# Fused attention and two feed-forward layers on one core: the projection of two heads placed in the two halves of the matmul array

## The chip, the cores and the metric

The kernel runs on one core of one Trainium2 chip. The metric is the device time of one execution in microseconds (us). Before the change the median of three runs is 1108.83 us (1107.52 to 1109.21). A profile comes from one separate execution, which took 1109.95 us; its span, from the first to the last recorded instruction, is 1108.2 us.

## The reference

Three layers follow one another. The first is linear attention with an exponential feature map (4 batches, 8 heads, 576 positions, head size 64, 128 features):

```python
def phi(x):
    proj = np.einsum('bhsd,df->bhsf', x, w_phi)
    proj = proj - np.max(np.abs(proj), axis=-1, keepdims=True)
    return np.concatenate([np.exp(proj), np.exp(-proj)], axis=-1)
q_p, k_p = phi(q), phi(k)
kv = np.einsum('bhsf,bhsd->bhfd', k_p, v)
z = np.sum(k_p, axis=2)
num = np.einsum('bhsf,bhfd->bhsd', q_p, kv)
den = np.einsum('bhsf,bhf->bhs', q_p, z)[..., None] + 1e-06
return num / den
```

The second takes the real part of a two-dimensional Fourier transform of the result (over 576 positions and 512 features), adds it, normalizes each row and adds `relu(un @ w_ch1) @ w_ch2` with 2048 hidden columns. The third normalizes again, with a gain, and adds a second such pair of products. The weights of both pairs come in double precision, and all sums are in single precision.

## The kernel before, in words

**Attention.** The work goes by 16 units of two heads of one batch. A tile `qk` of a unit (lines 99 to 114) has 128 rows, 64 for each of its two heads, and nine column tiles of 128 positions: four of q, one mixed tile (64 positions of q and 64 of k), and four of k. `project` (lines 116 to 132) multiplies such a tile, which is loaded into the array as weights, with `wbd`, a 128 x 256 matrix that has `w_phi` twice on its diagonal, zeros elsewhere: one matmul gives the 128 features of both heads. It is called five times for each unit, as q0, q1, k0 and k1 (two column tiles each) and mix (one). VectorE then takes the largest magnitude (line 125) and subtracts it (line 131). Matmuls on `F32` tiles come as two pairs of a weight load and a matmul each, transposes as one pair.

`k_exp` makes the exponentials on ScalarE (line 140). `kv` (lines 143 to 158) sums over positions: 20 matmuls for a unit, each with one position tile of exponentials as weights and the 65 columns of one head's `v` (64 and a column of ones) streamed. Its last four use 64 of the array's rows. ScalarE copies the sum to `z` (line 157). `q_exp` (lines 160 to 170) transposes the projected q, one piece of 64 rows (`ptc`, line 162) and four of 128 (`ptq`, line 165), and makes its exponentials. `num` (lines 172 to 201) streams the 65 columns of `z` past ten weight loads for each head; VectorE divides and writes the result to `ub` and `uc`.

**Order.** The list `rounds` (line 559) gives the order of these stages in a round; `num` belongs to the unit before, `load` to the second next. The stage `dft` stands for pieces of other work that are tied to a round (lines 532 to 544): the Fourier transform of finished batches (`fold`, `seq_stage`, `dim_stage`) and the decoding of the first weights. A planner that simulates the engines orders the instructions of each engine's queue from this program order and from what each waits for; the queues themselves run in order.

**PSUM.** Results of TensorE go to rings of banks by tag (line 48): `p` has two banks (projections, `ptc`, and later `ph`), `t` two (transposes), `n` four (`pk`, `px`, `pb`, `pd`, and later `acc`).

**Weights.** A block of raw weights (512 KB) is requested by SyncE in `fetch` (lines 314 to 323) into one of `RAW = 2` buffers `wraw`, and `decode` (lines 345 to 361) makes two single-precision tiles of it on ScalarE and VectorE; `decode` calls `fetch` itself. The first eight blocks are decoded in the rounds of line 532, the others at fixed places of the feed-forward loop (lines 493 to 498).

**Feed-forward.** From about 290 us on, `mm1` (line 427) and `mm2` (line 443) run for two layers, four groups of hidden columns and five chunks of rows; they are not touched by the change except by the rings and by the weights.

Of the kernel before, what the change touches and what calls it, by code (L numbers as in the profile page):

```python
# [19 lines left out]
F = 128  # L20
# [11 lines left out]
def fused_kernel(ctx, tc, qk_c, v_c, w_phi, w1s, w2s, g_ln, cs_c, cd_c, perm_c, out):  # L32
# [14 lines left out]
    def ps_tile(tag, shape, name):  # L47
        return psum.tile(shape, F32, tag=tag, bufs={"p": 2, "t": 2, "n": 4}[tag], name=name)
# [48 lines left out]
    KT = {"q0": 0, "q1": 2, "mix": 4, "k0": 5, "k1": 7}  # L97

    def load(u):
        qk = apool.tile([P, 9, P], F32, tag="qk", bufs=2, name="qk")  # L100
        vv = apool.tile([P, 5, 2, D + 1], F32, tag="vv", bufs=2, name="vv")
        def part(a, b):
            nc.sync.dma_start(qk[:, a:b], qk_c[u, :, a * P : b * P].rearrange("p (t c) -> p t c", c=P))

        if u == 0:
            part(5, 7)
            load_consts()
            part(7, 9)
            part(4, 5)
# [4 lines left out]
        st[u]["qk"], st[u]["v"] = qk, vv  # L114

    def project(u, name):
# [7 lines left out]
        mx = apool.tile([P, 2 * n], F32, tag="mx", bufs=4, name="mx")  # L124
        nc.vector.tensor_reduce(out=mx, in_=pp, op=ALU.max, axis=AX.X, apply_absolute_value=True)  # L125
        if name == "k0":
            st[u]["mx"] = mx[:, 0:1]
            if u == 0:
                load_dft_consts()
        t = bpool.tile([P, 2 * n, F], F32, tag="pm" + name[0], bufs=2, name="pm")  # L130
        nc.vector.tensor_tensor(out=t, in0=pp, in1=mx.unsqueeze(2).to_broadcast([P, 2 * n, F]), op=ALU.subtract)  # L131
        st[u]["pm", name] = t

    def k_exp(u, name):
        t = st[u]["pm", name]
        n = 1 if name == "mix" else 2
        r = slice(64, P) if name == "mix" else slice(0, P)
        e = apool.tile([P, 2 * n, 2, F], F32, tag=f"ek{n}", bufs=2, name="ek")
        for sgn in range(2):
            nc.scalar.activation(e[r, :, sgn], t[r], AF.Exp, scale=1.0 - 2.0 * sgn)  # L140
        st[u]["ek", name] = e

    def kv(u):
        pk = ps_tile("n", [P, 4, D + 1], "pk")
        first = True
        for t in range(5):
            e = st[u]["ek", ("k0", "k1", "mix")[t // 2]]
            r = slice(64, P) if t == 4 else slice(0, P)
            for j in range(2):
                for sgn in range(2):  # L150
                    nc.tensor.matmul(  # L151
                        pk[:, 2 * j + sgn, :], e[r, 2 * (t % 2) + j, sgn], st[u]["v"][r, t, j],
                        start=first, stop=(t == 4), skip_group_check=True,
                    )
                    first = False
        z = bpool.tile([P, 4, D + 1], F32, tag="z", bufs=2, name="z")
        nc.scalar.copy(z, pk)
        st[u]["z"] = z

    def q_exp(u, j):  # L160
        ptc = ps_tile("p", [P, 64], "ptc")
        nc.tensor.transpose(ptc, st[u]["pm", "mix"][0:64, j, :], ident[0:64, 0:64])
        pt = ps_tile("t", [P, 4, P], "ptq")
        for t in range(4):
            nc.tensor.transpose(pt[:, t, :], st[u]["pm", f"q{t // 2}"][:, 2 * (t % 2) + j, :], ident)  # L165
# [137 lines left out]
    weights = {}  # L303
    wpools = {}
# [9 lines left out]
    def fetch(layer, g, n):  # L314
# [8 lines left out]
        return raw  # L323
# [21 lines left out]
    def decode(layer, g, n):  # L345
# [4 lines left out]
        raw = fetch(layer, g, n)  # L350
# [123 lines left out]
    def moe(last_dft):  # L474
# [44 lines left out]
    nc.vector.memset(ub[0][:, 0], 0.0)  # L519
    warm = ps_tile("n", [P, DM], "warm")  # L520
# [11 lines left out]
    for n, step in enumerate((2, 3, 4, 7, 8, 11, 15, 17)):  # L532
        at(step, decode, 0, 0, n)
# [3 lines left out]
    for b in range(B - 1):  # L537
# [9 lines left out]
        "k0": lambda u: (project(u, "k0"), k_exp(u, "k0")),  # L547
        "k1": lambda u: (project(u, "k1"), k_exp(u, "k1")),
        "mix": lambda u: (project(u, "mix"), k_exp(u, "mix")),
        "q0": lambda u: project(u, "q0"),  # L550
        "q1": lambda u: project(u, "q1"),
# [8 lines left out]
        ("k0", 0), ("num0", -1), ("k1", 0), ("mix", 0), ("num1", -1), ("q0", 0),  # L560
        ("q1", 0), ("load", 2), ("dft", 0), ("e0", 0), ("kv", 0), ("e1", 0),
# [103 lines left out]
```

## Time and profile before

| | |
|---|---|
| median of the runs | 1108.83 us |
| profiled execution, its span | 1109.95 us, 1108.2 us |
| TensorE (PE) busy | 1086.3 us, 98% |
| weight loads (PEld) busy | 927.9 us, 84% |
| VectorE (DVE) busy | 615.0 us, 55% |
| ScalarE (ACT) busy | 340.5 us, 31% |
| GpSimd (POOL) busy | 45.3 us, 4% |

A row of a group of instructions gives line, engine, operation, written and read tiles, rows x columns of the array in use (128*64, 64*128), shape and count, then busy us and the mean ns of one, then idle time of the engine before it. A row of the timeline gives the start in us, the length in us from the first start to the last end, the engine and the instructions that it merges (x count). Matmuls are pipelined: of several in a row the distance between starts is the length less that of one, divided by the count less one. A row of windows gives for a stretch its length and the busy time of PE, PEld, DVE, ACT and POOL with counts, then PEclk, the granted clock of TensorE as a share of full speed, then the DMA share and GB/s. A row of waits gives who waited for whom: us in total, times, the longest.

### The profile page before, as it was taken

To read this page: it belongs to the slowest core of one execution; us is meant where nothing else is said; L and a number is where in the kernel's file an instruction comes from. 1 tells how busy PE (TensorE), PEld (TensorE's weight loads), DVE (VectorE), ACT (ScalarE), POOL (GpSimd) and SP (SyncE) were. 2 spreads that over 40 slices of the span, in tenths; PEclk is the share of its full clock that TensorE was granted. 3 is DMA by queue.
4 is the path that set the end of the run, shared out by engine and by line. 5 is a ranking of instruction groups with operands and counts; after the bars stand their busy time and mean duration, and the time that the engine had idled before them with its cause. 6 is when DMAs were issued, how large, how long until landed. Compare 5 with 4: busy or idle time off the path is not lost.

```text
span 1108.2 us, 14381 instructions
## 1 busy us (share of the span) xinstructions
PE 1086.3 (98%) x5806; PEld 927.9 (84%) x5806; DVE 615.0 (55%) x1315; ACT 340.5 (31%) x682; POOL 45.3 (4%) x53
## 2 busy tenths in 40 slices
PE   9899999999999999999999999999999999999996
PEld 7789989999788888888888788888878888888885
DVE  5897586774879476238327755762383264222131
ACT  4545454454435131113113343521231132011110
POOL 1000020300210000000000000000000000000010
PEclk9899999999999999999999999999999999999998
DMA  7452121110003122003101300220031011000111
GB/s 257 144 161 77 46 60 42 57 46 1 1 1 114 39 76 76 1 1 114 39 1 50 103 1 1 64 89 1 1 115 38 1 39 38 1 1 10 48 48 67
DMA packets 19755, 57.26 MB, mean 52 GB/s; under 512 B 2728, under 2 KB 3432, under 8 KB 19432
## 3 DMA queue, kind: packets, MB, share of 16 engines
q1 hardware_dynamic: 18536, 51.01, 14.3%
q0 software_dynamic: 1008, 5.19, 1.3%
q8 instruction: 46, 0.75, 0.3%
q14 instruction: 21, 0.17, 0.1%
q10 hardware_dynamic: 144, 0.13, 0.0%
HBM read 51.60 MB, written 4.72 MB: 51 GB/s over the span
## 4 chain that ended last, share of the span: by engine, by line
PE 86%; DVE 8%; DMA 4%; ACT 2%; issue 1%; POOLq 0%; POOL 0%; DVEq 0%; SPq 0%; ACTq 0%
PE acc L443 33%; PE ph L427 32%; PE pk L151 5%; PE px L181 5%; PE pp L121 5%; DMA wraw<-in_moe_w_ch 4%; PE pb L260 2%; PE ptq L165 1%; PE ptx L409 1%; PE pd L287 1%; DVE wm L342 1%; DVE wm L337 1%; DVE xx L215 1%; DVE wm L334 0%; DVE hl L431 0%
## 5 line engine op out<-in xcount | busy, mean ns | idle before, releaser
L427 PE MATMUL ph<-xth,wh 128*128 128x512 f32 (+1 forms) x640 | 236.2, 369 | 0.7 <-ACT xth L411 0.7
L427 PE MATMUL ph<-xtl,wh 128*128 128x512 f32 (+1 forms) x640 | 235.8, 368 | 0.0
L427 PE MATMUL ph<-xth,wl 128*128 128x512 f32 (+1 forms) x640 | 235.7, 368 | 0.0
L431 DVE SCALAR_TENSOR_TENSOR hl<-ph,hh 128x512 fp32r<-128x512 f32 (+1 forms) x160 | 101.5, 634 | 232.7 <-ACT hh L430 232.4
L430 ACT ACTIVATE hh<-ph 128x512 fp32r<-128x512 f32 (+1 forms) x160 | 88.4, 554 | 461.6 <-PE ph L427 456.4
L443 PE MATMUL acc<-wl,hh 128*128 128x512 f32 x576 | 224.2, 390 | 0.0
L443 PE MATMUL acc<-wh,hh 128*128 128x512 f32 x576 | 221.2, 391 | 2.5 <-ACT hh L430 2.5
L443 PE MATMUL acc<-wh,hl 128*128 128x512 f32 x576 | 195.3, 390 | 0.0
L427 PEld LDWEIGHTS ph<-xth,wh 128*128 128x128 f32 x640 | 120.4, 188 | 21.8 <-ACT xth L411 0.9
L427 PEld LDWEIGHTS ph<-xtl,wh 128*128 128x128 f32 x640 | 120.5, 188 | 20.7
L427 PEld LDWEIGHTS ph<-xth,wl 128*128 128x128 f32 x640 | 120.6, 188 | 20.0
L445 DVE TENSOR_TENSOR u<-acc,u 128x512 f32<-128x512 f32 x128 | 81.2, 682 | 94.3 <-PE acc L443 94.1
L443 PEld LDWEIGHTS acc<-wh,hh 128*128 128x128 f32 x576 | 108.1, 188 | 25.4 <-ACT hh L430 3.6
L443 PEld LDWEIGHTS acc<-wl,hh 128*128 128x128 f32 x576 | 108.2, 188 | 22.1
L443 PEld LDWEIGHTS acc<-wh,hl 128*128 128x128 f32 x576 | 107.1, 188 | 21.2
L121 PE MATMUL pp<-wbd,qk 128*128 128x256 f32 x288 | 80.2, 398 | 3.2 <-ACT eq L168 1.9
L151 PEld LDWEIGHTS pk<-vv,ek 128*128 128x128 f32 (+1 forms) x640 | 77.6, 191 | 5.2 <-ACT ek L140 1.8
L151 PE MATMUL pk<-vv,ek 128*128 128x65 f32 (+1 forms) x640 | 80.1, 273 | 0.8 <-ACT ek L140 0.6
L181 PEld LDWEIGHTS px<-z,eq 128*128 128x128 f32 (+1 forms) x640 | 76.3, 186 | 3.9 <-issue 0.3
L181 PE MATMUL px<-z,eq 128*128 128x65 f32 (+1 forms) x640 | 76.1, 268 | 0.0
L125 DVE TENSOR_REDUCE mx<-pp 128x4 f32<-128x512 f32 (+1 forms) x80 | 50.5, 631 | 45.5 <-PE pp L121 44.8
L140 ACT ACTIVATE ek<-pm 128x512 f32<-128x512 f32 (+1 forms) x96 | 48.2, 551 | 44.5 <-DVE pm L131 44.2
(100 smaller groups left out, 954.2 us busy)
## 6 DMA issues: line engine op xcount, KB each, us to landing
wraw<-in_moe_w_ch SPq DMA_DIRECT2D x64, 512.0 KB
vv<-in_v SPq DMA_DIRECT2D x16, 325.0 KB
qk<-in_qk SPq DMA_DIRECT2D x15, 320.0 KB
qk<-in_qk SPq DMA_DIRECT2D x16, 256.0 KB
out<-u SPq DMA_DIRECT2D x8, 256.0 KB
cs<-c_seq POOLq DMA_DIRECT2D x1, 1920.0 KB, 10.3
cd<-c_dim POOLq DMA_DIRECT2D x1, 1032.0 KB, 13.0
out<-uc SPq DMA_DIRECT2D x4, 126.0 KB
```

Of the source, the lines that this page charges most:

```text
L121: nc.tensor.matmul(pp[:, 2 * i : 2 * i + 2, :], qk[:, KT[name] + i], wbd.rearrange("p h f -> p (h f)"), start=True, stop=True)
L125: nc.vector.tensor_reduce(out=mx, in_=pp, op=ALU.max, axis=AX.X, apply_absolute_value=True)
L140: nc.scalar.activation(e[r, :, sgn], t[r], AF.Exp, scale=1.0 - 2.0 * sgn)
L151: nc.tensor.matmul(pk[:, 2 * j + sgn, :], e[r, 2 * (t % 2) + j, sgn], st[u]["v"][r, t, j], start=first, stop=(t == 4), skip_group_check=True,)
L165: nc.tensor.transpose(pt[:, t, :], st[u]["pm", f"q{t // 2}"][:, 2 * (t % 2) + j, :], ident)
L181: nc.tensor.matmul(px[0 : c.stop - c.start, t, :], e[:, sgn, c], z[:, 2 * j + sgn], start=(t == 0 and sgn == 0), stop=(sgn == 1), skip_gro ...
L260: nc.tensor.matmul(o, a, c, start=(n == 0), stop=(n == len(mm) - 1), skip_group_check=(m == 2))
L427: nc.tensor.matmul(ph[:, 0:n], a[:, kk, sl], x[:, kk], start=(i == 0), stop=(i == 11))
L430: nc.scalar.activation(hh[:, 0:n], ph[:, 0:n], AF.Relu)
L431: nc.vector.scalar_tensor_tensor(out=hl[:, 0:n], in0=ph[:, 0:n], scalar=0.0, in1=f32(hh[:, 0:n]), op0=ALU.max, op1=ALU.subtract)
L443: nc.tensor.matmul(acc, x[:, sl], w[:, f], start=(f == 0 and n == 0), stop=(f == 3 and n == 2))
L445: nc.vector.tensor_tensor(out=x, in0=acc, in1=x, op=ALU.add)
```

## The change

The two heads of a unit are projected by separate matmuls. For q and for k each, four position tiles times two heads make eight matmuls; each uses the 64 array rows of its head, and streams the 128 columns of `w_phi` instead of 256. The results of the two heads go to two banks, and `center` (the maximum and the subtraction) is called once for each head. The mixed tile stays as it was. The first unit's k tiles are now loaded by one request.

The ring `p` gets three banks, `n` three, and `ptc` moves from `p` to `n`. `kv` streams 128 columns instead of 65, 63 of which belong to the other head and are not used; `z` is copied by two instructions; `num` streams 102 columns instead of 65, of which 65 are used.

`fetch` is taken out of `decode`. For the first group it is called one round before its `decode`; for the other groups the next block's `fetch` stands in front of a block's `decode`. The number of buffers stays two.

```diff
-        return psum.tile(shape, F32, tag=tag, bufs={"p": 2, "t": 2, "n": 4}[tag], name=name)
+        return psum.tile(shape, F32, tag=tag, bufs={"p": 3, "t": 2, "n": 3}[tag], name=name)
...
         if u == 0:
-            part(5, 7)
+            part(5, 9)
             load_consts()
-            part(7, 9)
             part(4, 5)
...
     def project(u, name):
-        n = 1 if name == "mix" else 2
+
         qk = st[u]["qk"]
-        pp = ps_tile("p", [P, 2 * n, F], "pp")
-        for i in range(n):
-            nc.tensor.matmul(
-                pp[:, 2 * i : 2 * i + 2, :], qk[:, KT[name] + i], wbd.rearrange("p h f -> p (h f)"), start=True, stop=True
-            )
...
+        pp = [ps_tile("p", [P, 4, F], "pp") for _ in range(2)]
+        for i in range(4):
+            for j in range(2):
+                r = slice(j * D, (j + 1) * D)
+                nc.tensor.matmul(pp[j][:, i], qk[r, KT[name] + i], wbd[r, j], start=True, stop=True)
+        for j in range(2):
+            mx = center(u, name, j, pp[j])
...
     def kv(u):
-        pk = ps_tile("n", [P, 4, D + 1], "pk")
+
+        pk = ps_tile("n", [P, 4, P], "pk")
...
                     nc.tensor.matmul(
-                        pk[:, 2 * j + sgn, :], e[r, 2 * (t % 2) + j, sgn], st[u]["v"][r, t, j],
+                        pk[:, 2 * j + sgn, :], e[r, sgn], st[u]["v"][r, t].rearrange("p h d -> p (h d)")[:, 2 * j : 2 * j + P],
                         start=first, stop=(t == 4), skip_group_check=True,
...
-        z = bpool.tile([P, 4, D + 1], F32, tag="z", bufs=2, name="z")
-        nc.scalar.copy(z, pk)
+        z = zs[u % 2]
+        for j in range(2):
+            c = slice(j * (D - 1), j * (D - 1) + D + 1)
+            nc.scalar.copy(
+                z[:, 2 * j * (D + 1) : 2 * (j + 1) * (D + 1)].rearrange("p (s d) -> p s d", s=2),
+                pk[:, 2 * j : 2 * j + 2, c],
+            )
...
+    ZW = 102
+    zs = [bpool.tile([P, 3 * (D + 1) + ZW], F32, name=f"z{i}") for i in range(2)]
...
-        ptc = ps_tile("p", [P, 64], "ptc")
+        ptc = ps_tile("n", [P, 64], "ptc")
...
-        px = ps_tile("n", [P, 5, D + 1], "px")
+        px = ps_tile("n", [P, 5, ZW], "px")
...
-                    px[0 : c.stop - c.start, t, :], e[:, sgn, c], z[:, 2 * j + sgn],
+                    px[0 : c.stop - c.start, t, :], e[:, sgn, c],
+                    z[:, (2 * j + sgn) * (D + 1) : (2 * j + sgn) * (D + 1) + ZW],
...
-        for k in range(8):
-            side.setdefault((0, 2 + k // 4, 2 * (k % 4)), []).append(partial(decode, 0, 1, k))
-        for p in range(1, 7):
-            for k in range(8):
-                at = (p, k // 2, 1 + 4 * (k % 2))
-                side.setdefault(at, []).append(partial(decode, (p + 1) // 4, (p + 1) % 4, k))
+        def weight_steps(p, times):
+
+            blocks = [((p // 4, p % 4, k), t) for k, t in enumerate(times)]
+            side.setdefault(blocks[0][1], []).insert(0, partial(fetch, *blocks[0][0]))
+            for (a, t), nxt in zip(blocks, blocks[1:] + [None]):
+                side[t] = side.get(t, []) + ([partial(fetch, *nxt[0])] if nxt else []) + [partial(decode, *a)]
+
+        weight_steps(1, [(0, 2 + k // 4, 2 * (k % 4)) for k in range(8)])
+        for p in range(2, 8):
+            weight_steps(p, [(p - 1, k // 2, 1 + 4 * (k % 2)) for k in range(8)])
...
     for n, step in enumerate((2, 3, 4, 7, 8, 11, 15, 17)):
+        at(step - 1, fetch, 0, 0, n)
         at(step, decode, 0, 0, n)
...
     rounds = (
-        ("k0", 0), ("num0", -1), ("k1", 0), ("mix", 0), ("num1", -1), ("q0", 0),
-        ("q1", 0), ("load", 2), ("dft", 0), ("e0", 0), ("kv", 0), ("e1", 0),
+        ("k", 0), ("num0", -1), ("mix", 0), ("num1", -1), ("q", 0),
+        ("load", 2), ("dft", 0), ("e0", 0), ("kv", 0), ("e1", 0),
     )
```

## Rows read from the trace of the kernel before

**Rows 1.** The page's first part: busy us, share of span, instructions.

```profile
PE 1086.3 (98%) x5806; PEld 927.9 (84%) x5806; DVE 615.0 (55%) x1315; ACT 340.5 (31%) x682; POOL 45.3 (4%) x53
```

**Rows 2.** Windows: attention, and the feed-forward part.

```profile
0.00:290.00 290.00, 282.18 (x2006) 255.32 (x2007) 211.66 (x520) 142.56 (x333) 32.05 (x39) 0.99 0.26 85
...
340.00:1108.00 768.00, 755.58 (x3557) 632.71 (x3556) 361.86 (x694) 176.55 (x305) 7.80 (x8) 1.00 0.13 41
```

**Rows 3.** Waits of TensorE, over the whole span.

```profile
PE acc L443 <- ACT hh L430: 2.5, 2, 1.4
PE ptc L162 <- ACT eq L168: 2.0, 1, 2.0
PE pp L121 <- ACT eq L168: 1.9, 4, 0.6
```

**Rows 4.** Groups by line with shapes apart: projections and the two sums.

```profile
L121 PE MATMUL pp<-wbd,qk 128*128 128x256 f32 x288 | 80.2, 398 | 3.2 <-ACT eq L168 1.9 <-PE pp L121 0.7 <-issue 0.6
...
L181 PE MATMUL px<-z,eq 128*128 128x65 f32 x576 | 70.0, 272 | 0.0
L151 PE MATMUL pk<-vv,ek 128*128 128x65 f32 x512 | 62.9, 272 | 0.8 <-ACT ek L140 0.6
...
L181 PE MATMUL px<-z,eq 128*64 128x65 f32 x64 | 7.3, 234 | 0.0
```

**Rows 5.** Timeline of TensorE: one projection matmul, three, and eleven of a sum.

```profile
182.85 0.38 PE L121 MATMUL pp<-wbd,qk 128*128 128x256 f32 x1
...
114.48 0.81 PE L121 MATMUL pp<-wbd,qk 128*128 128x256 f32 x3
...
115.75 1.39 PE L181 MATMUL px<-z,eq 128*128 128x65 f32 x11
```

**Rows 6.** Timeline of TensorE: four matmuls with 64 weight columns.

```profile
19.14 0.45 PE L181 MATMUL px<-z,eq 128*64 128x65 f32 x4
```

**Rows 7.** Timeline of TensorE: a 64-row transpose between 128-row instructions.

```profile
93.75 0.50 PE L151 MATMUL pk<-vv,ek 128*128 128x65 f32 x3
94.19 0.27 PE L162 MATMUL ptc<-perm,pm 64*128 64x64 f32 x1
94.39 0.44 PE L165 MATMUL ptq<-perm,pm 128*128 128x128 f32 x2
```

**Rows 8.** Timeline: a transpose in rows 0-63 among matmuls in rows 64-127.

```profile
181.48 0.61 PE L151 MATMUL pk<-vv,ek 64*128 64x65 f32 x4
181.82 0.27 PE L162 MATMUL ptc<-perm,pm 64*128 64x64 f32 x1
181.93 0.38 PE L151 MATMUL pk<-vv,ek 64*128 64x65 f32 x2
...
181.82 0.14 PEld L162 LDWEIGHTS ptc<-perm,pm 64*128 64x128 f32 x1
```

**Rows 9.** Timeline: the one such place with another order of starts.

```profile
29.20 0.13 PEld L162 LDWEIGHTS ptc<-perm,pm 64*128 64x128 f32 x1
29.22 0.19 PEld L151 LDWEIGHTS pk<-vv,ek 64*128 64x128 f32 x1
29.23 0.24 PE L162 MATMUL ptc<-perm,pm 64*128 64x64 f32 x1
```

**Rows 10.** Window of the one low stretch of the clock in attention.

```profile
46.30:53.10 6.80, 4.94 (x15) 3.93 (x15) 5.15 (x11) 4.45 (x13) 0.00 (x0) 0.50 0.44 152
```

**Rows 11.** Windows: a stretch with decoding, and one with little beside attention.

```profile
70.00:90.00 20.00, 19.41 (x145) 17.60 (x144) 19.74 (x52) 10.91 (x24) 5.01 (x2) 1.00 0.41 126
160.00:200.00 40.00, 39.92 (x293) 36.63 (x294) 23.08 (x61) 20.23 (x53) 0.00 (x0) 1.00 0.20 62
```

**Rows 12.** Waits of SyncE's queue; timeline of ScalarE in the feed-forward part.

```profile
SPq L322 <- DVE wm L342: 694.4, 62, 96.5
...
622.37 0.67 ACT L329 ACTIVATE wm<-wraw 128x512 f32<-128x512 f32 x1 [1.79 <-DMA wraw<-in_moe_w_ch]
```

**Rows 13.** Groups by line: the copy of the sum.

```profile
L157 ACT COPY z<-pk 128x260 f32<-128x260 f32 x16 | 6.0, 377 | 21.1 <-PE pk L151 21.1
```

More of the change, by code (lines that the diff above doesn't have):

```diff
@@ L96, in fused_kernel @@
     st = [dict() for _ in range(NUNIT)]
-    KT = {"q0": 0, "q1": 2, "mix": 4, "k0": 5, "k1": 7}
+    KT = {"q": 0, "mix": 4, "k": 5}
     def load(u):
@@ L114, in load, with center @@
         st[u]["qk"], st[u]["v"] = qk, vv
+    def center(u, name, j, pp):
+        n = pp.shape[1]
+        mx = apool.tile([P, n], F32, tag="mx", bufs=4, name="mx")
+        nc.vector.tensor_reduce(out=mx, in_=pp, op=ALU.max, axis=AX.X, apply_absolute_value=True)
+        t = bpool.tile([P, n, F], F32, tag="pm" + name[0], bufs=2, name="pm")
+        nc.vector.tensor_tensor(out=t, in0=pp, in1=mx.unsqueeze(2).to_broadcast([P, n, F]), op=ALU.subtract)
+        st[u]["pm", name, j] = t
+        return mx
@@ L126, in project @@
[L126 to L136, printed above, removed]
+        pp = [ps_tile("p", [P, 4, F], "pp") for _ in range(2)]
@@ new lines, in project, with project_mix @@
+        for i in range(4):
[4 more added lines that the diff above has]
+            mx = center(u, name, j, pp[j])
+            if name == "k":
+                st[u]["mx"] = mx[:, 0:1]
+                if u == 0:
+                    load_dft_consts()
+    def project_mix(u):
+        pp = ps_tile("p", [P, 2, F], "pp")
+        nc.tensor.matmul(pp, st[u]["qk"][:, KT["mix"]], wbd.rearrange("p h f -> p (h f)"), start=True, stop=True)
+        center(u, "mix", 0, pp)
@@ L137, in k_exp @@
+    def k_exp(u, name, j):
+        t = st[u]["pm", name, j]
         r = slice(64, P) if name == "mix" else slice(0, P)
-        e = apool.tile([P, 2 * n, 2, F], F32, tag=f"ek{n}", bufs=2, name="ek")
+        e = apool.tile([P, t.shape[1], 2, F], F32, tag="ek" + name[0], bufs=2, name="ek")
         for sgn in range(2):
             nc.scalar.activation(e[r, :, sgn], t[r], AF.Exp, scale=1.0 - 2.0 * sgn)
-        st[u]["ek", name] = e
+        st[u]["ek", name, j] = e
     def kv(u):
-        pk = ps_tile("n", [P, 4, D + 1], "pk")
+        pk = ps_tile("n", [P, 4, P], "pk")
@@ L155, in kv @@
                     first = False
-        z = bpool.tile([P, 4, D + 1], F32, tag="z", bufs=2, name="z")
-        nc.scalar.copy(z, pk)
+        z = zs[u % 2]
[5 more added lines that the diff above has]
+            )
         st[u]["z"] = z
+    ZW = 102
+    zs = [bpool.tile([P, 3 * (D + 1) + ZW], F32, name=f"z{i}") for i in range(2)]
     def q_exp(u, j):
-        ptc = ps_tile("p", [P, 64], "ptc")
-        nc.tensor.transpose(ptc, st[u]["pm", "mix"][0:64, j, :], ident[0:64, 0:64])
+        ptc = ps_tile("n", [P, 64], "ptc")
+        nc.tensor.transpose(ptc, st[u]["pm", "mix", 0][0:64, j, :], ident[0:64, 0:64])
         pt = ps_tile("t", [P, 4, P], "ptq")
         for t in range(4):
-            nc.tensor.transpose(pt[:, t, :], st[u]["pm", f"q{t // 2}"][:, 2 * (t % 2) + j, :], ident)
+            nc.tensor.transpose(pt[:, t, :], st[u]["pm", "q", j][:, t, :], ident)
         e = bpool.tile([P, 2, S], F32, tag="eq", bufs=2, name="eq")
@@ L303, in fused_kernel @@
     weights = {}
+    raws = {}
     wpools = {}
@@ L349, in decode @@
         wh, wl = weights[layer, g][w]
-        raw = fetch(layer, g, n)
+        raw = raws.pop((layer, g, n))
         m = to_float(raw)
@@ L519, in fused_kernel @@
     nc.vector.memset(ub[0][:, 0], 0.0)
+    for z in zs:
+        nc.vector.memset(z[:, 4 * (D + 1) :], 0.0)
     warm = ps_tile("n", [P, DM], "warm")
@@ L546, in fused_kernel @@
         "load": load,
[L547 to L551, printed above, removed]
+        "k": lambda u: (project(u, "k"), k_exp(u, "k", 0), k_exp(u, "k", 1)),
+        "mix": lambda u: (project_mix(u), k_exp(u, "mix", 0)),
+        "q": lambda u: project(u, "q"),
         "e0": lambda u: q_exp(u, 0),
```

6 lines of the change are left out of this document (2 added, 4 removed).

## Prediction

> **What bounds the kernel now.** I read the first part of the page, then the windows by stage, then the waits of TensorE, then its timeline for the distances between starts. The page says that TensorE is busy for 1086.3 of 1108.2 us [rows 1]; the windows say the same of each stage: 282.2 of the 290 us of attention, 755.6 of 768 of the feed-forward part [rows 2]. Busy time overlaps from one matmul to the next, so I check it by the waits: the longest of TensorE are 2.5, 2.0 and 1.9 us in total [rows 3]. The reader is to see that hardly any time goes to waiting: TensorE's stream of instructions sets the time, and an edit counts by what it does to the distance between their starts. Only attention changes there: 288 projection matmuls, 640 of `px`, and 640 of `pk`, of which 512 with all rows [rows 4].
>
> **Projection: the streams.** One projection matmul lasts 0.38 us and three 0.81, so starts are (0.81 - 0.38)/2 = 0.215 us apart for 256 columns [rows 5]. A run of eight (two calls of `project`) takes 8 x 0.215 = 1.72 us. Streaming a column thus costs 0.215/256 = 0.00084 us: 128 columns 0.108, 102 columns 0.086, 65 columns 0.055. Yet eleven `px` matmuls of 65 columns take 1.39 us with 0.27 for the last: starts 0.112 apart [rows 4, 5]. So there the load of 128 weight columns sets the pace, at 0.112; with 64 weight columns four take 0.45, the last 0.23 [rows 4, 6], about 0.07 apart.
>
> The changed projection has 16 matmuls in that run, each with its own load of 128 columns and a stream of 0.108. Loads set 0.112 in each half of the array, eight for each half. If the halves run beside one another, the run takes 8 x 0.112 + one offset of 0.112 = 1.01 us, a gain of 0.71; if not, 16 x 0.112 = 1.79, a loss of 0.07, or a little less loss where part overlaps. These are the two ends.
>
> **Projection: changes between whole and half array.** A 64-row transpose between 128-row work starts 0.21 us after the matmul before it, and the next starts 0.20 after it, where 0.11 is usual, and the one after that is 0.165 behind (0.44 - 0.27) where 0.11 is usual [rows 4, 7]. So a change costs 0.09 + 0.055 = 0.15 us. A longer stream ahead of it drains longer (102 or 128 columns for 65: 0.03 to 0.05), so I take 0.18. Each run needs a change in and one out: 0.36 of the 0.71. There are 32 such runs (q and k of 16 units): 32 x 0.35 = 11.2 us gained. Where a run stands beside `ptc` or the last `pk` matmuls, which are 64-row too, a change is saved; at most one for each run, 4.8 us. I take none.
>
> **Do the halves overlap?** At 181.8 us `ptc`, in rows 0 to 63, starts in the middle of `pk` matmuls in rows 64 to 127. The last `pk` before it starts at 181.48 + 0.61 - 0.27 = 181.82, the next at 181.93: they keep their 0.11, and `ptc` ends with the former at 182.09. Its load, too, starts at 181.82 between theirs [rows 8]. So loads and streams of two halves do run together, for one transpose. What isn't shown is that they stay together in a row. The two passes of head 0 come before those of head 1, so the second matmul of head 0 waits for the first; the load for head 1 has to pass that waiting matmul. In 13 of the 14 places like this the other half's load starts only after the matmul before it has started, as here. In one, a `pk` load starts at 29.22 ahead of the `ptc` matmul at 29.23 that stands before it in the program [rows 9]. The 13 loads carry a semaphore wait, which the projection's don't; so I side with the one, at about six in ten.
>
> The Trainium skill, "TensorE: Matmul & The Clock Gate", Part 3 (The mechanism), says that the engine pulls a weight load ahead of matmuls whose row group doesn't conflict. By that rule the run is the 1.01 us above in every case; by the 13 places alone it would be the first rival below. No run here shows the rule for two loads in a row.
>
> **Wider sums.** For `pk` (128 columns, 0.108) and the 576 full `px` (102 columns, 0.086) the load still sets 0.112: nothing, hidden under the load. If a load could not run under a stream, each would cost up to 0.05 more, some 60 us over 1216; but the projections' 0.215 holds stream and load in one [rows 5], so I exclude it. The 64 `px` with 64 weight columns go from 0.07 or less to 0.086: 64 x 0.02 = 1.3 us. At the changes there are now (in and out of the last `pk`, into the short `px`) the longer stream drains: 48 x 0.05 = 2.4. Together 3.7 us lost.
>
> **Rings.** The waits of `ptc` and `pp` on `eq` (3.9 us) [rows 3] are for the ring `p`, where `ptc` held a bank; there they go. What is late next is the ring `n`, which loses a bank and takes in `ptc`, beside `px`, `pk`, `pb` and pairs of `pd`. I put new waits between 0 and 4 us and take 2, a gain of 2. The clock was granted at half for 6.8 us from 46.3 on [rows 10], right after the 2.0 us wait, which costs 3.4 us of stream. If the wait goes, so may that; I take 2 of the 3.4, and as the other end one more such stretch.
>
> **Raw weights.** SyncE waits 694 us, 62 times, for VectorE to free a `wraw` buffer [rows 12], and there are two buffers before and after. A request further ahead in the queue waits for the same buffer, so I take nothing. What it could bring at most is the 2.5 us that TensorE waits on `hh` [rows 3], where ScalarE stood 1.79 us on a block [rows 12]; lost could be as much, where a request that waits for its buffer delays the `qk` request behind it in SyncE's queue.
>
> **VectorE.** Its work is the same but for the pieces: 211.7 of 290 us in attention [rows 2]. But in stretches with decoding or transform work it is full, 19.7 of 20 us; elsewhere it has room, 23.1 of 40 [rows 11]. Some 80 of the 290 us are like the former, and a quarter of the net gain (7.5) is lost there: 2 us. The second copy to `z` adds at most the 0.38 of the present one for each unit on ScalarE [rows 13]; `num` needs it a round later, so nothing. If ScalarE were late it would be 16 x 0.38 = 6 us. The first unit's one request is hidden by the warm-up matmuls; at worst 0.7 us.
>
> **The sum**, from the profiled 1109.95 us: - 11.2 + 3.7 - 2 - 2 + 2 = -9.5, so 1100.4; the runs' median is 1.1 below the profiled execution, so 1099.5.
>
> **The rivals.**
> 1. The halves don't stay together: either the load waits behind the blocked matmul, or the streams take turns. Then the run is 1.79 us and the changes between whole and half array are pure loss: 32 x (0.07 + 0.36) = 13.8, with the sums 17.5, less 4 for rings and clock: 13.5 slower, 1122 on the runs' scale. It decides from about 1.4 us for a run. For: the 13 places. Against: rows 9, and that streams do overlap.
> 2. VectorE takes the place of TensorE. It must subtract a bank pair before the next projection, in three banks; if it holds the gain down to the quiet third of attention, 2.5 us are left of 7.5 and the rings give nothing back: 1106 to 1109. For: full stretches. Against: 27% of attention idle. The Trainium skill, "TensorEngine Tiling (Array Packing)", PSUM Bottleneck, says that array packing speeds up the matmuls and not the emptying of PSUM, which may become the bound; the full stretches agree, their neighbours don't.
> 3. All goes well: no low clock, no ring waits, 2.5 us of the weights' wait gone, some changes shared: 1109.95 - 11.2 + 3.7 - 3.9 - 3.4 - 2.5 - 3 = 1090, 1089 on the runs' scale.
>
> **How the numbers follow.** Forecast 0.50 (1093 to 1105), rival 1 0.28 (1113 to 1127), rival 2 0.12, rival 3 0.10 (1087 to 1093). A measurement of this kernel tells 0.2%, 2.2 us, from no change. Faster: 0.49 + 0.10 + 0.03 = 0.62; same 0.01 + 0.07 = 0.08; slower 0.28 + 0.02 = 0.30. The range leaves out half of rival 1 and most of rival 3: 1091 to 1121; the forecast's own is 1093 to 1105.
>
> **What would show it.** In the changed profile a run of 16 projection matmuls should take about 1.0 us from first to last start (rival 1: 1.7 or more), starts before and after it 0.2 to 0.3 apart, `px` and `pk` still 0.112, `ptc` and `pp` without waits on `eq`, attention ending 8 to 10 us earlier, and the feed-forward part as long as now, with its two waits. I am wrong if the run's length is near 1.7, if `px` and `pk` starts move beyond 0.12, if new low stretches of the clock appear, or if waits on `n` banks exceed 4 us.

## The result, and the profile after

The changed kernel takes 1121.2 us (median of four runs, 1120.33 to 1121.8) against 1109.02 for the kernel before on the same chip: a ratio of 1.0105, 95% interval 1.0089 to 1.0121. It is 12 us slower where 9.5 us faster were forecast. Executions differ in how long TensorE's clock stands at its lower level, so one profiled execution can lie several us from its kernel's median, and ratios leave out executions over 1.5% above their kernel's fastest. The profiled one here took 1121.2.

The first part of the page and the two windows, answering to [rows 1, 2]:

```profile
PE 1093.5 (98%) x6062; PEld 930.4 (83%) x6062; DVE 617.5 (55%) x1317; ACT 337.6 (30%) x698; POOL 45.1 (4%) x58
...
0.00:290.00 290.00, 275.74 (x2160) 244.02 (x2161) 197.10 (x495) 133.58 (x335) 25.90 (x39) 0.98 0.29 96
340.00:1119.00 779.00, 772.46 (x3640) 647.58 (x3638) 387.02 (x749) 186.02 (x323) 10.06 (x11) 1.00 0.13 42
```

TensorE now stands idle for 14.3 of the first 290 us, where it was 7.8 before. The waits of TensorE, answering to [rows 3], name the place:

```profile
PE ptc L181 <- DMA perm<-c_perm: 6.8, 1, 6.8
PE pp L132 <- DVE pm L121: 3.7, 3, 1.4
PE pb L280 <- DVE xs L246: 1.9, 1, 1.9
PE ph L448 <- DVE hl L452: 1.9, 1, 1.9
...
PE ptc L181 <- DVE rr L313: 1.2, 1, 1.2
```

No `ptc` or `pp` waits for `eq` any more, as forecast; but the longest wait is one that the prediction does not contain. The DMA issues of the page and the one instruction tell why (first two: count, KB each, us to landing; third: ns that issuing took, first and last start in us):

```profile
cs<-c_seq POOLq DMA_DIRECT2D x2, 1920.0 KB, 8.2
cd<-c_dim POOLq DMA_DIRECT2D x2, 1032.0 KB, 9.2
...
L75 SPq DMA_DIRECT2D perm<-c_perm x2: 327/334/340, 4.3 to 9.5; - x2
```

The tables are requested twice. `load_dft_consts()` stood in `project`, guarded by `name == "k0"`; the change moved it into the loop over the two heads, where `name == "k"` and `u == 0` hold twice. The first transpose must wait until the second copy of `perm`, issued at 9.5 us, has landed among 3 MB of tables that are sent again. The timeline of TensorE at that place, and the windows of the low clock, the first of which begins within that wait:

```profile
17.43 0.34 PE L181 MATMUL ptc<-perm,pm 64*128 64x64 f32 x1 [6.82 <-DMA perm<-c_perm]
```
```profile
12.40:22.60 10.20, 5.17 (x21) 4.63 (x22) 0.02 (x1) 0.68 (x4) 1.45 (x4) 0.50 1.04 415
155.80:159.10 3.30, 3.30 (x18) 3.30 (x17) 3.30 (x9) 0.91 (x2) 3.30 (x3) 0.50 0.02 7
312.80:316.10 3.30, 3.30 (x14) 2.58 (x13) 3.15 (x10) 0.75 (x2) 0.74 (x2) 0.50 0.00 0
```

The clock was granted at half (1.2 of 2.4 GHz) in three stretches of 16.8 us together, beside one behind the last matmuls in every kernel; before it was one of 6.8 [rows 10].

And the projections? The forecast hung on runs of 16 half-array matmuls in 1.01 us. Timeline of TensorE, one run early in the attention and two halves of later ones:

```profile
33.16 1.16 PE L132 MATMUL pp<-wbd,qk 64*128 64x128 f32 x16
...
54.84 1.16 PE L132 MATMUL pp<-wbd,qk 64*128 64x128 f32 x8
...
72.00 1.16 PE L132 MATMUL pp<-wbd,qk 64*128 64x128 f32 x8
```

With 0.27 for the last matmul, the first row is 16 matmuls in 0.89 us from first to last start, the starts alternately 7 and 105 ns apart but for one step of 206 near the beginning: the halves do run beside one another. The others are 8 matmuls in the same 0.89 us, the first two 0.213 apart and the rest 0.112: one head alone. The program order alternates the heads, but the planner gives out a matmul when its bank is free, and a projection takes two of the three banks of ring `p`, with `mix` between. Only seven stretches have just 16 in a row, four of them in 0.89 us. Of the 256 starts that would come under 40 ns behind another if all were paired, 113 do. That the order of the queue parts the halves is tested below (3).

**A ledger.** Busy times overlap, so I add up distances: for each kernel, the distance from the start of each matmul in the trace to the start of the next, put down to the tile of the first. In stretches at half clock (a distance belongs to one if it starts in it) half of each distance goes to the tile and half to "low clock". Outside them, a distance over 0.33 us leaves 0.2 with the tile and the rest in "waits"; the warm-up is left whole. "Ends" is what lies before the first and behind the last start. So each column adds up to the span of the one profiled execution (us):

| | before | after | single request | whole array | pair of banks | before, wide | before, end |
|---|---|---|---|---|---|---|---|
| `pp` | 62.8 | 62.2 | 63.9 | 66.5 | 42.5 | 61.3 | 62.5 |
| `ptc`, `ptq` | 22.2 | 20.7 | 20.3 | 19.5 | 22.3 | 22.3 | 22.1 |
| `pk` | 73.2 | 75.8 | 74.9 | 75.1 | 74.9 | 76.6 | 73.3 |
| `px` | 70.0 | 75.0 | 74.9 | 73.8 | 75.1 | 73.0 | 70.2 |
| `pb`, `pd`, `ptx` | 57.9 | 59.1 | 59.0 | 58.3 | 58.4 | 58.2 | 57.9 |
| `ph`, `acc`, warm-up | 792.4 | 792.3 | 792.2 | 792.2 | 792.3 | 792.3 | 792.3 |
| low clock | 2.7 | 6.0 | 10.2 | 3.2 | 9.9 | 1.6 | 3.3 |
| waits | 14.9 | 19.5 | 12.0 | 8.5 | 25.2 | 15.0 | 16.8 |
| ends | 12.0 | 8.8 | 8.9 | 8.9 | 12.0 | 11.9 | 7.0 |
| span | 1108.2 | 1119.4 | 1116.2 | 1105.9 | 1112.6 | 1112.2 | 1105.4 |

The columns from the third on are experiments, below, in this order: the tables requested once (1), projections over all 128 rows and a pair of banks for them (3), the kernel before with the wide sums (4) and with another end (5).

### The profile page after: what moved, and what is told of

The parts are those of the page before. It is cut to its first block, busy times and chain, and to the rows that moved or that the text cites. A ratio compares the mean times of both kernels' runs of the same rounds, so it can differ in the third digit from the quotient of the medians.

```text
span 1119.4 us, 14918 instructions
## 1 busy us (share of the span) xinstructions
PE 1093.5 (98%) x6062; PEld 930.4 (83%) x6062; DVE 617.5 (55%) x1317; ACT 337.6 (30%) x698; POOL 45.1 (4%) x58
## 4 chain that ended last, share of the span: by engine, by line
PE 93%; DVE 3%; DMA 2%; ACT 1%; issue 0%; POOLq 0%; ACTq 0%; DVEq 0%
PE ph L448 35%; PE acc L464 35%; PE pk L162 7%; PE px L200 6%; PE pp L132 4%; PE pb L280 2%; PE ptq L184 1%; PE ptx L430 1%; DMA perm<-c_perm 1%; PE pp L142 1%; DVE u L317 1%; PE pd L307 1%; DVE xx L235 0%; DMA wraw<-in_moe_w_ch 0%; ACT ek L150 0%
## 5 line engine op out<-in xcount | busy, mean ns | idle before, releaser
L464 PE MATMUL acc<-wl,hh 128*128 128x512 f32 x576 | 220.7, 390 | 0.0
L464 PE MATMUL acc<-wh,hh 128*128 128x512 f32 x576 | 218.6, 391 | 0.0
L464 PE MATMUL acc<-wh,hl 128*128 128x512 f32 x576 | 211.4, 390 | 0.0
L466 DVE TENSOR_TENSOR u<-acc,u 128x512 f32<-128x512 f32 x128 | 85.6, 687 | 137.2 <-PE acc L464 136.9
L162 PE MATMUL pk<-vv,ek 128*128 128x128 f32 (+1 forms) x640 | 82.3, 286 | 0.3 <-ACT qs L311 0.2
L200 PE MATMUL px<-z,eq 128*128 128x102 f32 (+1 forms) x640 | 77.4, 276 | 0.3 <-ACT z L170 0.3
L200 PEld LDWEIGHTS px<-z,eq 128*128 128x128 f32 (+1 forms) x640 | 72.9, 186 | 4.5 <-ACT z L170 0.5
L132 PE MATMUL pp<-wbd,qk 64*128 64x128 f32 x512 | 59.1, 290 | 4.2 <-DVE pm L121 3.7
L132 PEld LDWEIGHTS pp<-wbd,qk 64*128 64x128 f32 x512 | 49.0, 189 | 14.8 <-issue 9.3
```

The costliest lines, as they stand in the source:

```text
L132: nc.tensor.matmul(pp[j][:, i], qk[r, KT[name] + i], wbd[r, j], start=True, stop=True)
L162: nc.tensor.matmul(pk[:, 2 * j + sgn, :], e[r, sgn], st[u]["v"][r, t].rearrange("p h d -> p (h d)")[:, 2 * j : 2 * j + P], start=first, st ...
L200: nc.tensor.matmul(px[0 : c.stop - c.start, t, :], e[:, sgn, c], z[:, (2 * j + sgn) * (D + 1) : (2 * j + sgn) * (D + 1) + ZW], start=(t == ...
L464: nc.tensor.matmul(acc, x[:, sl], w[:, f], start=(f == 0 and n == 0), stop=(f == 3 and n == 2))
L466: nc.vector.tensor_tensor(out=x, in0=acc, in1=x, op=ALU.add)
```

## Experiments

Each was timed in turns with the kernel before; the ratio is to that, with its 95% interval. It is not the quotient of the medians.

**1. The double request.** Two kernels from both sides.

```diff
-                if u == 0:
+                if u == 0 and j == 0:
                     load_dft_consts()
```

> The changed kernel, but the cosine tables, alt and perm are requested once, after the first head's maximum of unit 0, not once for each head. Theory A (the second request is the loss: 6.8 us of the first transposes on perm, the half clock of 10.2 us behind it, and everything after it moved back): 8 to 11 us faster than the changed kernel, 1110 to 1113 us, the first unit's last px sum 9 to 10 us earlier; the feed-forward keeps its 3 to 4 us. Theory B (rival 1 of the prediction, the runs that are split by head and their mode changes are the loss, the second request lies beside other work): 0 to 3 us faster, 1118 to 1121 us, the delay of the first unit made up for by the runs of the later units in which TensorE waits less.

Measured: 1116.1 us, 1.0065 (1.0044 to 1.0087), 5.1 us faster than the changed kernel.

```diff
             if u == 0:
                 load_dft_consts()
+                load_dft_consts()
```

> The kernel before, but cosine tables, alt and perm are requested twice in unit 0, one request right behind the other, as in the changed kernel. Theory A: 7 to 11 us slower than the kernel before, 1116 to 1120 us, the first transposes waiting 5 us or more for perm. Theory B: within 3 us of the kernel before, 1109 to 1112 us.

Measured: 1114.35 us, 1.0081 (1.0049 to 1.0112), 5.3 us slower than before. Its first waits show the same place, shorter:

```profile
PE ptc L163 <- DMA perm<-c_perm: 2.4, 1, 2.4
```

So by the medians the double request costs about 5 us from both sides. By the ratios its size is less sure: 4.4 us less on the changed kernel, 5.4 to 12.4 more on the kernel before. The first is short of theory A's 8 us, the second beyond theory B's 3. The other 7 us of the loss have another cause.

**2. The raw blocks requested ahead,** alone on the kernel before, with the function `weight_steps` of the change, and taken out of the kernel with the single request.

```diff
-        raw = fetch(layer, g, n)
+        raw = raws.pop((layer, g, n))
...
+        at(step - 1, fetch, 0, 0, n)
```

> The kernel before with one part of the change alone: raw weight blocks are requested one round before they are decoded. Theory A (it is this that gives the feed-forward back 3 to 4 us, the two waits for weights near 622 and 694 us being gone): 2 to 4 us faster than before, 1105 to 1107 us, with the attention as long as before. Theory B (the shorter feed-forward comes from the different start of the stage, or the wider rings): within 1 us of before, 1108 to 1110 us.

Measured: 1108.7 us, 0.9992 (0.9975 to 1.0009).

```diff
         wh, wl = weights[layer, g][w]
+        fetch(layer, g, n)
         raw = raws.pop((layer, g, n))
...
-        at(step - 1, fetch, 0, 0, n)
```

> The kernel of the single request of the tables, with the request of each raw weight block back beside its decoding: so the halves, the wide sums and the rings alone. Theory A: 2 to 4 us slower than the kernel of the single request (1112 to 1116 us), the feed-forward waiting for weights again near 622 and 694 us after its start of the stage; and 3 to 6 us slower than the kernel before, since the runs that are split by head gain nothing and pay mode changes and longer sums. Theory B (the request ahead is worth nothing): within 1 us of the kernel of the single request.

Measured: 1118.47 us, 1.0079 (1.0058 to 1.0101), an interval that overlaps that of the single request. Theory A falls: on the kernel before nothing can be measured, and the waits of `acc` for `hh` [rows 3] stay there, 1.8 us, while they are gone in the kernel without the early request. (In the kernel before they stand at 622 and 828 us, not near 694.) What shortens the end of the kernel is something else (5).

**3. The halves.** First without them: each head's projection with all 128 rows, 128 columns a matmul, all else as with the single request.

```diff
-                r = slice(j * D, (j + 1) * D)
-                nc.tensor.matmul(pp[j][:, i], qk[r, KT[name] + i], wbd[r, j], start=True, stop=True)
+                nc.tensor.matmul(pp[j][:, i], qk[:, KT[name] + i], wbd[:, j], start=True, stop=True)
```

> The kernel of the single request, but each head's projection takes all 128 rows (its weights' other half is zero), 128 columns a matmul, so nothing runs in halves; rings, sums and raw requests stay. Theory A (the halves as they now run, mostly one head at a time, gain no more than their changes of mode cost): within 3 us of the kernel of the single request, 1113 to 1118 us, a run of 16 at 16 x 0.112 = 1.8 us. Theory B (the halves do gain several us, and something else costs more): 5 to 10 us slower, 1121 to 1126 us.

Measured: 1107.78 us, 0.9993 (0.9981 to 1.0006): 8.3 us faster than with halves. Both theories missed; neither had the halves as a loss of that size. The ledger splits it: without halves `pp` costs 2.6 us more, `ptc` and `ptq` 0.8 less, the low clock takes 7.0 less and waits 3.5 less. The two profiles are one execution each; the granted clock of all executions goes the same way, on the mean 0.991 of six with halves and 0.996 of twelve without. The low stretches in the kernel with halves:

```profile
10.90:17.70 6.80, 6.80 (x32) 6.13 (x30) 2.29 (x4) 2.55 (x9) 0.00 (x0) 0.50 0.96 389
92.80:96.20 3.40, 3.40 (x19) 3.40 (x18) 3.39 (x8) 0.00 (x0) 0.35 (x1) 0.50 0.67 200
229.40:236.10 6.70, 6.14 (x25) 5.12 (x25) 6.59 (x19) 2.27 (x6) 1.71 (x3) 0.50 0.00 0
301.00:304.40 3.40, 3.31 (x8) 2.64 (x9) 3.40 (x8) 0.00 (x0) 0.00 (x0) 0.50 0.00 0
```

TensorE is nearly always busy in them, but its starts are about twice as far apart: 32 in the first 6.8 us. They follow distances of 1.7, 1.2, 1.5 and 2.3 us between starts. The whole-array kernel has two stretches of 3.4, behind distances of 1.9 and 2.3.

Then with all halves paired: both heads in one tile of two banks.

```diff
-        bufs={"p": 3, "t": 2, "n": 3}[tag]
+        bufs={"p": 1, "t": 2, "n": 4}[tag]
...
-        pp = [ps_tile("p", [P, 4, F], "pp") for _ in range(2)]
+        pp = ps_tile("p", [P, 2, 4, F], "pp")
...
-        ph = ps_tile("p", [P, 512], "ph")
+        if not phs:
+            phs.append(ps_tile("p", [P, 2, 512], "ph"))
+        ph = phs[0][:, f % 2]
```

> The kernel of the single request, with both heads of a projection in one tile of two banks, so that no order can part them (rings p one tile of two banks, t 2, n 4 as before the change; the mix projection is in ring n, the feed-forward keeps two banks for ph). Theory A (the prediction's 11 us of the projections failed because most runs were given out one head at a time, at 0.112 us a matmul): every run of 16 takes 0.9 to 1.0 us from first to last start, the projections fall by 10 to 14 us of TensorE's time, 1102 to 1108 us. Theory B (the halves are paid for elsewhere: half clock, VectorE, changes of mode): the runs do become short, but 1112 to 1118 us, TensorE waiting for VectorE's pm at the projections instead.

Measured: 1180.24 us, 1.0627 (1.0604 to 1.0651). This one misled: I had put `ph` of the feed-forward into two slices of a single tile, and `acc` then waits 39.1 us for `hh`. Mended, with two banks for `ph` from a pool opened when the attention's is closed:

```diff
-        if not phs:
-            phs.append(ps_tile("p", [P, 2, 512], "ph"))
-        ph = phs[0][:, f % 2]
+        ph = ps_tile("h", [P, 512], "ph")
```

> As the kernel with both heads in one tile of two banks, but with the feed-forward's ph in two banks of its own, opened when the attention's are closed, so that the 39 us of acc waiting for hh go. Theory A (with all runs paired the halves gain, what is left against the kernel before is half clock and waits for the one pair of banks): attention 5 to 7 us longer than before, feed-forward as before, 1113 to 1118 us. Theory B (the pair itself is worth its 11 us once nothing else is changed): 1102 to 1108 us.

Measured: 1114.91 us, 1.0051 (1.003 to 1.0073), theory A. Its projections, beside those of the changed kernel, each in the first 290 us (busy us, mean ns; idle before):

```profile
L135 PE MATMUL pp<-wbd,qk 64*128 64x128 f32 x512 | 41.3, 296 | 10.9 <-issue 7.3 <-DVE pm L124 2.5 <-PE px L203 1.1
```
```profile
L132 PE MATMUL pp<-wbd,qk 64*128 64x128 f32 x512 | 59.1, 290 | 4.2 <-DVE pm L121 3.7 <-PE pp L142 0.5
```

Here 27 runs are whole, 22 of them in 0.89 us. Against the kernel before with wide sums, the nearest with the same banks, `pp` falls by 18.8 us; waits rise by 10.2 and low clock by 8.3. Nearly nothing is left: the span is 0.4 us longer, the median 1.4 shorter. One of the waits, on VectorE and TensorE:

```profile
159.93 1.01 DVE L122 TENSOR_REDUCE mx<-pp 128x4 f32<-128x512 f32 x2
...
161.06 1.00 DVE L124 TENSOR_TENSOR pm<-pp,mx 128x512 f32<-128x512 f32 x2
...
161.84 0.92 PE L135 MATMUL pp<-wbd,qk 64*128 64x128 f32 x11 [3.02 <-issue]
```

The page finds no releaser, but the neighbours point to one: the first of the two subtractions is the last from the only pair (the other is the mixed tile's); it ends at 161.73, and TensorE starts the next pair at 161.84. So I gave it two pairs, with two banks left in ring `n`, and `mix` and `ptc` in ring `t`:

```diff
-        bufs={"p": 1, "h": 2, "t": 2, "n": 4}[tag]
+        bufs={"p": 2, "h": 2, "t": 2, "n": 2}[tag]
```

> As the kernel with the pair of banks and ph in banks of its own, but two pairs (4 banks) for the projections, mix and ptc in ring t, 2 banks left in ring n. Theory A (with one pair, TensorE's 17 us at the projections are given back as waits of the next projection for VectorE, 7 to 9 us, and as half clock): the waits of pp fall under 3 us, 1105 to 1111 us. Theory B (VectorE's reductions or two banks for the sums bound the stage instead): the waits move to px and pk, 1113 us or more.

Measured: 1124.3 us, 1.013 (1.0096 to 1.0164). `pp` waits less, 3.3 us in the ledger instead of 12.4, so the one pair of banks was what it waited for. But the waits of the ledger rise from 25.2 to 33.9, now mostly at `ph` (8.6), `acc` (6.9) and `pd` (4.7), and `pp` itself takes 47.8 us, with 13 whole runs for 27. So theory B has the time, but at other tiles: `acc` and `pd` have two banks instead of four; why `ph` waits is not shown. In neither of the two splits of the eight banks do the pairs keep what they save.

**4. The wide sums,** taken out of the kernel with the single request:

```diff
-        pk = ps_tile("n", [P, 4, P], "pk")
+        pk = ps_tile("n", [P, 4, D + 1], "pk")
...
-    ZW = 102
+    ZW = 65
```

> The kernel of the single request, with the sums back at 65 columns. Theory A (the wide sums cost what the prediction gave them, 3.7 us): 2 to 5 us faster, 1111 to 1114 us, px of 64 rows back at 0.06 us. Theory B (their columns lie under the weight loads, which take 0.111 us at either width): within 1.5 us of it, 1115 to 1117 us. Theory C (the wide sums hold TensorE's clock up, and narrow ones let it fall): slower, 1118 to 1122 us, with more than 20 us at the lower clock.

Measured: 1172.42 us (1151.17 to 1180.83), 1.0438 (1.0379 to 1.0497). Theory C, far beyond its size. Two of its stretches:

```profile
11.00:79.00 68.00, 65.50 (x320) 59.91 (x318) 45.15 (x107) 27.31 (x63) 0.30 (x2) 0.50 0.50 165
...
110.00:157.70 47.70, 45.80 (x230) 43.17 (x231) 22.28 (x48) 12.85 (x32) 2.35 (x1) 0.50 0.12 39
```

In all 164 us were granted at half clock, 81 us of loss in the ledger. The same edit with whole-array projections of 128 columns:

> Projections with all rows at 128 columns, and sums of 65 columns. Theory A (the granted clock falls where halves and narrow sums come together; whole-array projections keep it up): under 25 us at half clock, 1103 to 1110 us, as the kernel with wide sums or 3 us faster. Theory B (it is the narrow sums alone that let the clock fall, whatever the projections are, once these stream 128 and no longer 256 columns): over 60 us at half clock, 1135 us or more.

Measured: 1110.9 us (1102.69 to 1113.82), 0.9986 (0.9958 to 1.0014), with 23.9 us at half clock in the profiled execution of 1112.08: theory A, but for the time. At a mean granted clock of 0.996 or 0.997, which five of the twelve executions had, it took 1102.7 to 1104.5 us, some 3 us less than the whole-array kernel with wide sums and near the prediction's term of 3.7. The wide sums alone, on the kernel before (`kv`, `zs` and `num` as in the change):

```diff
-        px = ps_tile("n", [P, 5, D + 1], "px")
+        px = ps_tile("n", [P, 5, ZW], "px")
```

> The kernel before with the wide sums alone. Theory A (the prediction's term): 2 to 5 us slower, 1111 to 1114 us, px of 64 rows 0.087 us instead of 0.06, the rest of the sums at 0.112 us as before. Theory B (the wide sums cost nothing that shows, since they take away the half-clock stretch of 6.8 us, 3.4 us): within 1.5 us of the kernel before.

Measured: 1116.32 us, 1.0063 (1.0044 to 1.0081); the profiled execution is 4.0 us above that of before, the medians 7.6; theory A is the nearer, and too low. `pk` and `px` cost 6.3 us more in the ledger, the low clock 1.1 less. The 64 short `px` start 0.105 us apart on the mean instead of 0.077 (1.3 us in all), and the full `pk` and `px` 0.114 and 0.111 instead of 0.1085. That mean hides two kinds: nine in ten start 0.11 apart with either width, but 76 full ones, each the second of its group, started about 0.06 us behind the first before, and now start 0.087 (`px`) or 0.108 and more (`pk`) behind it. Two such, before and with wide sums:

```profile
101.92 0.33 PE L181 MATMUL px<-z,eq 128*128 128x65 f32 x2
```
```profile
100.56 0.36 PE L190 MATMUL px<-z,eq 128*128 128x102 f32 x2
```

With 0.275 for the second, the starts are 0.057 and 0.087 apart: there the stream sets the distance, not the load. These places are about half of the 6.3 us.

**5. The rings, and the end.**

```diff
-        bufs={"p": 2, "t": 2, "n": 4}[tag]
+        bufs={"p": 3, "t": 2, "n": 3}[tag]
```

> The kernel before with the rings alone changed: p 3 banks and n 3 instead of 2 and 4 (ptc and everything else as before). Theory A (the shorter feed-forward of the changed kernel comes from the third bank of ring p, which ph uses there): the two waits of acc for hh are gone and the feed-forward is 2.5 to 4 us shorter; if the attention keeps its length, 1105 to 1107 us. Theory B (it comes from something else in the change): the waits stay, 1108 to 1110 us, or slower where three banks of ring n hold the attention up (1111 or more).

Measured: 1107.45 us (1105.16 to 1127.18), 0.9998 (0.9971 to 1.0026). Inconclusive in time: the profiled execution took 1117.47 with 30.7 us at half clock. But the two waits of `acc` for `hh` are gone with the rings alone, and so is part of the end: 7.3 us from the last matmul's start to the end of the span, 10.5 before. With wide sums as well:

> The kernel before with the wide sums and the rings of 3, 2 and 3 banks. Theory A (the rings of 3, 2 and 3 banks lower TensorE's clock in some executions by 24 us of half clock, as in the profiled one of the kernel with these rings alone; wide sums hold it up): all runs within 3 us of each other, at 1104 to 1108 us. Theory B (the sums do nothing for the clock there): some runs at 1116 us and above again, the others at 1106 to 1110 us.

Measured: 1115.83 us (1114.54 to 1120.31), 1.0065 (1.004 to 1.009). Neither theory: all runs lie within 5.8 us, but 8 to 12 us higher than A said. The end is 7.3 us here too. So not the third bank of `p` but the missing fourth of `n` is its likely cause, and it can be had alone:

```diff
-        acc = ps_tile("n", [P, DM], "acc")
+        acc = ps_tile("t" if (layer, g, c) == (1, 3, B - 1) else "n", [P, DM], "acc")
```

> The kernel before with one change behind the attention: the four acc tiles of the very last chunk are taken from the two banks of ring t, not the four of ring n, so that two of them are finished and stored before the other two. Theory A (the 3.1 us that the feed-forward of the changed kernel seemed to gain lie behind the last matmul: with four banks all four tiles end together, and their adds and stores follow one another): the time behind the last matmul falls from 10.5 to 7 to 8.5 us, 1105.5 to 1107.5 us. Theory B (the last store is bound by the transfer alone): within 0.7 us of before.

Measured: 1105.44 us, 0.9967 (0.9943 to 0.999): faster than both kernels. Behind the last matmul's start are 5.6 us instead of 10.5. The order of all instructions ahead of the last chunk is that of the kernel before, but for two starts of `ptc` and `pk` that change places at 29 and at 64 us. The last adds of VectorE, before and in this kernel:

```profile
1096.51 2.48 DVE L445 TENSOR_TENSOR u<-acc,u 128x512 f32<-128x512 f32 x4 [4.80 <-PE acc L443]
```
```profile
1093.74 1.29 DVE L445 TENSOR_TENSOR u<-acc,u 128x512 f32<-128x512 f32 x2 [1.62 <-PE acc L443]
1097.54 0.69 DVE L445 TENSOR_TENSOR u<-acc,u 128x512 f32<-128x512 f32 x1 [2.52 <-PE acc L443]
1100.26 0.69 DVE L445 TENSOR_TENSOR u<-acc,u 128x512 f32<-128x512 f32 x1 [2.03 <-PE acc L443]
```

With four banks the planner lets all four tiles grow together, so they end together, and four adds and their stores queue up behind the last matmul. With fewer banks only the last one does. Then `ptc` in ring `n`, as in the changed kernel:

```diff
-        ptc = ps_tile("p", [P, 64], "ptc")
+        ptc = ps_tile("n", [P, 64], "ptc")
```

> As that kernel, and ptc in ring n as in the changed kernel. Theory A (the waits of ptc and pp for eq, 3.9 us, and the half-clock stretch behind the longest of them, 3.4 us, are what ring p costs): 1101 to 1104 us. Theory B (ptc then waits in ring n, or the clock falls elsewhere): 1105 to 1109 us.

Measured: 1121.93 us, 1.0084 (1.0049 to 1.012). Both theories missed: the waits on `eq` do go, others come (18.0 us in the ledger for 16.8), and the clock is low for 44.3 us in the profiled execution, the longest of seven (1114.08 to 1128.96):

```profile
36.30:60.20 23.90, 22.79 (x92) 19.23 (x92) 12.78 (x36) 6.46 (x16) 0.00 (x0) 0.50 0.29 97
166.00:176.20 10.20, 10.20 (x41) 8.43 (x40) 6.29 (x30) 3.81 (x7) 0.00 (x0) 0.50 0.00 1
237.60:247.80 10.20, 10.20 (x46) 9.50 (x45) 6.06 (x18) 3.64 (x9) 0.98 (x2) 0.50 0.11 33
```

## Why the prediction was wrong

The terms against the ledger, the kernel of the single request less the kernel before; the double request stands by itself:

| step | predicted | measured |
|---|---|---|
| first unit's requests | at most 0.7 | 5.1 and 5.3 (medians) |
| projections | -11.2 | +1.1 |
| changes of mode shared with `ptc`, `pk` | 0 (at most -4.8) | not separated |
| `ptc`, `ptq` | not foreseen | -1.9 |
| wider sums | +3.7 | +6.5 |
| waits (rings and VectorE) | -2 + 2 | -2.9 |
| low clock | -2 | +7.4 |
| raw blocks | 0 | nothing measurable |
| the end | not foreseen | -3.1 |
| `pb`, `pd`, `ptx` | not foreseen | +1.1 |

The fall of `ptc` and `ptq` is no shared change of mode: the whole-array kernel has none to share with its projections, and there they take 19.5, still less. The forecast's last step has a slip: 1100.4 less 1.1 is 1099.3, not 1099.5.

**The part of the change that I read wrongly.** "The first unit's one request is hidden by the warm-up matmuls": I looked at the request of `qk`, and did not follow what else the moved lines issue. Once in a loop over heads, the call runs twice; about 5 of the 12 us hang on it.

**Projections: the premise, not the arithmetic.** The step that failed is "32 x 0.35 = 11.2 us gained", for its 32. Whole runs take 0.89 us, less than the 1.01 forecast, for the halves start 7 ns apart where an offset of 0.112 was allowed. The Trainium skill, "TensorE: Matmul & The Clock Gate", Part 3 (The mechanism), says that loads whose row group doesn't conflict are pulled ahead. The trace agrees, for sixteen in a row: in the run at 33.16 us the loads for both halves' second matmuls start at 33.26 and 33.27, these matmuls at 33.37 and 33.38, so the second half's load passes the first half's matmul. Where all runs are paired `pp` falls by 18.8 to 20.3 us, more than forecast. But in the changed kernel most runs come one head at a time, 16 x 0.112 as in rival 1, and pay changes of mode: +1.1 us in the ledger. Rival 1 had the length of these runs for a wrong reason: the order in which the matmuls are given out parts the halves, not the array. That its price (1122) is met is luck: it gave the projections 13.8 us, and the rest of the loss came from the double request, the low clock and the sums, which it had lower or not at all. I had written "what isn't shown is that they stay together" and asked the hardware alone; the three banks of ring `p` stood in the diff.

**Clock: the sign.** I counted the one low stretch [rows 10] as tied to one wait and likely to go with it. It did not begin behind that wait, as I read it, but within it, so 2.7 us hung on it and not 3.4. The kernel with halves had more: 20.4 us at half clock with them and 6.8 without, and with narrow sums 163.9 and 23.9. It is, after the projections, the term that was furthest off; the granted clocks of all executions and the medians, 8.3 us apart with the wide sums, go the same way. In the profiles of the kernel before, the changed one and those of the single request, the whole array and the mended pair, all 14 low stretches begin in or shortly behind a distance of 1.2 to 7.1 us between starts; but not each such distance has one behind it (1.5 us at 44.6 and 1.4 at 150.8 of the single request have none).

**Wider sums: the size.** "Hidden under the load" was right for nine in ten of the full sums. It missed the second of many a group, where the stream set the distance, about 0.06 us before (4). The other bound that I excluded, 0.05 each, stays excluded.

**Rings and VectorE.** The waits of `ptc` and `pp` on `eq` went, as forecast; with the single request `pk` waits 2.2 us for `eq` in their place, near the 2 that I took. Rival 2 is what the paired kernel shows, not the changed one: of TensorE's gain 10.2 us come back as waits, most of them for the one pair of banks that VectorE has to empty, and 8.3 as low clock. The Trainium skill, "TensorEngine Tiling (Array Packing)", PSUM Bottleneck, which that rival cited, says that packing does not speed up the emptying of PSUM. The trace of the paired kernel agrees, with 12.4 us of waits at `pp` and 3.3 with two pairs.

**Raw blocks** are worth nothing that can be measured, by the argument given: two buffers before and after. **Feed-forward** "as long as now, with its two waits" was wrong: the waits are gone and the end is 3.1 us shorter, both also with the rings alone, which I had weighed for attention only.

What stays open: why `ptc` in ring `n` brings so much low clock, and whether the low stretches follow from the waits ahead of them or from what runs between. So the 7.4 us of low clock are measured, and their cause is not shown. Each kernel's order by the planner differs, so no run here changes the clock alone.

## What to carry to other kernels

Before costing a moved line, count how often it runs in its new place, and what it issues. An overlap that needs two instructions side by side is worth only what the order of the queue gives it: look up which buffers both need, and whether there are enough to force the pair. Where an engine is busy throughout, add up start-to-start distances with low clock and waits apart: busy time is 98% of the span before and after, and the terms of this case can't be read from it.

## What was not expected of the hardware

- Sums of 65 columns and the clock: in four pairs of kernels that differ in the sums' width (in the first two also in the copy to `z`), the wide one's profile has less time at half clock: 3.4 for 6.8 us (before), 10.2 for 30.7 (with the rings), 6.8 for 23.9 (whole array), 20.4 for 163.9 (halves). One profile each; the mean granted clock of all executions agrees for the last two (0.996 for 0.992, 0.991 for 0.930), less clearly with the rings (0.992 for 0.990), and not for the first (0.994 for both).
- Half-array matmuls in two row groups start 7 ns apart and keep 0.112 us each: sixteen in 0.89 us, with one step of 0.206 at the change into halves, and weight loads of 128 columns included.
- Not the hardware, but the order: fewer banks for the last chunk made a kernel faster, for its tiles ended one after another and 3 to 5 us less lay behind the last matmul.
